# Twenty-four short products of constant tiles placed among the first two attention jobs

## The chip, the cores and the metric

The kernel runs on one core of a Trainium2 chip. A core has five engines that run side by side, each through its own instructions in order: TensorE (PE, with its weight loads as PEld), VectorE (DVE), ScalarE (ACT), GpSimd (POOL) and SyncE (SP, which sends DMAs here). The metric is the time of one execution on the device in microseconds (us). The median of three timed runs of the kernel before is 696.04 us (694.4 to 696.12).

## The reference

Three layers follow each other:

```
# 1. attention, q, k, v: (2 batches, 8 heads, 576 positions, 64)
q_d, k_d, v_d = means over 4 neighbouring positions          # 144 positions
out = repeat(softmax(q_d k_d^T / 8) v_d, 4)                  # coarse part
    + softmax(q k^T / 8 where |i - j| < 4) v                 # band part
x = out as (1152 tokens, 512)
# 2. h = x @ w_in (512 x 2048);  x = (h * sigmoid(h)) @ w_out (2048 x 512)
# 3. p = domain_probs normalized over 4 experts
out = sum over e of p[:, e] * (relu(x @ w1[e]) @ w2[e])      # w1 512 x 1024, w2 1024 x 512
```

Everything is float32.

## The kernel before

**Work and stages.** Attention is cut into 16 jobs: 2 batches x 2 column blocks (`c`: 256 or 320 positions) x 4 pairs of heads (`hp`). A job j runs through these helpers: `local_scores` (band scores in windows of 64 positions, L318, and a product of a small identity `ident16` with the constant `mask`, L324, that adds the mask), `local_max` and `local_exp` (L331, L332, L336), `pool_kq_first` for the first four jobs (four products with `ident` that sum neighbouring keys into `kd`, L282, copied out by ACT, L285), `down_scores` (L342), `down_max` (L356 to L358), `norm` (L363 to L368), `trans` (transposes of both weights, L378 and L380), `values` (L406, L410, then L413 and L415) and `split_x` (L422, L423), which writes the job's part of x as an upper and a lower half, `xh` and `xl`. The tile `ps` of a job is one PSUM bank and holds both its kinds of scores.

The second layer, `g1_step` and `g2_step`, multiplies halves: xh by the upper weights, xl by the upper, xh by the lower (`mm3`, L485). The first three products over tokens of the first block are begun while attention still runs (`start_mm`, in PSUM tiles `hold`, of which it uses columns 0 to 255). The third layer (L673 to L719) follows.

**Weights.** The weights of the second layer come in eight units of four pieces of 512 KB. SP loads a piece into one of three stage buffers (`load_raw`, L154); `split_raw` takes it apart into two halves with ACT (L179, L180, L187), DVE (L181, L185) and POOL (L188), and frees the buffer. The splits of unit 1 are tied behind L423 of job 2, those of units 2 and 3 behind L423 of job 3 (`behind_job`).

**What sets the order.** The code issues steps by ticks (`plan_jobs`): job k starts at tick -18 + 3k; its down scores come 2 ticks later, its transposes 5, its values 6, its split 7. Each instruction gets a priority from its tick, and a scheduler with a model of times then writes each engine's order. `follow(i, earlier, ...)` adds an edge that keeps i behind `earlier` in that order, without a semaphore when both are on one engine; `after` is `follow` for two products in one PSUM bank.

Of the kernel before, what the change touches and what calls it, by code (L numbers as in the profile page):

```python
# [9 lines left out]
F32 = mybir.dt.float32  # L10
# [11 lines left out]
HP = NH // 2  # L22
# [4 lines left out]
WIN = BQ + 6  # L27
# [14 lines left out]
HOLD = 3  # L42
# [17 lines left out]
def attention_moe_kernel(ctx, tc, kqa, kqb, qtl, va, vb, w64, w1d, w2d, dpr, out):  # L60
    nc = tc.nc
    PE, ACT, DVE, POOL, SP = nc.tensor, nc.scalar, nc.vector, nc.gpsimd, nc.sync

    const = ctx.enter_context(tc.tile_pool(name="const", bufs=1))
    mm_p = ctx.enter_context(tc.tile_pool(name="mm", bufs=3, space=PSUM))
# [46 lines left out]
    def follow(i, earlier, reason):  # L112
        tc.add_manual_dep(i.ins, earlier.ins.name, mybir.DependencyInfo(mybir.DependencyClass.NoSync, mybir.DependencyReason.DATA),
                          reason=reason)
# [77 lines left out]
            behind(DVE, DVE.tensor_tensor(out=l[:, c], in0=t, in1=h[:, c].bitcast(F32), op=ALU.subtract))  # L192


    actx = ExitStack()
    ac = actx.enter_context(tc.tile_pool(name="ac", bufs=1))
    a2 = actx.enter_context(tc.tile_pool(name="a2", bufs=2))
# [5 lines left out]
    ident = ac.tile([128, 128], F32, name="ident")  # L203
    ident16 = ac.tile([128, 128], BF16, name="ident16")
    mask = ac.tile([128, 6, WIN], BF16, name="mask")
# [71 lines left out]
    def pool_kq_first(j):  # L277
        kp = j.ps[:, 352:352 + SD]
        kd[j.b, j.hp] = a4.tile([128, SD], F32, tag="kd", name="kd")
        k4 = j.k[:, 3:3 + S].rearrange("p (n r) -> p n r", r=4)  # L280
        for r in range(4):
            i = PE.matmul(out=kp, lhsT=ident, rhs=k4[:, :, r], start=(r == 0), stop=(r == 3))  # L282
            if r == 0:
                after(i, j.group)
        ACT.activation(out=kd[j.b, j.hp], in_=kp, func=ACTF.Copy)  # L285
        j.qd = qbd[j.hp % 2]
        q4 = j.q[:, 0:256].rearrange("p (n r) -> p n r", r=4)
        for h in range(2):
            p = slice(64 * h, 64 * h + 64)
            DVE.tensor_reduce(out=j.qd[p, h], in_=q4[p], axis=AX.X, op=ALU.add)  # L290
# [16 lines left out]
    def after(i, earlier):  # L307
        follow(i, earlier, "PSUM bank")

    def local_scores(j):  # L310
        nb = j.nb
        j.ps = s_p.tile([128, 512], F32, tag="s", name="s")
        mk = mask[:, 0:4] if j.c == 0 else mask[:, 1:6]
        first = [None, None]
        for m in range(nb):
            for h in range(2):
                p = slice(64 * h, 64 * h + 64)
                i = PE.matmul(out=j.ps[p, m * WIN:(m + 1) * WIN], lhsT=j.q[p, 64 * m:64 * m + 64],  # L318
                              rhs=j.k[p, 64 * m:64 * m + WIN], start=(m == 0), stop=False, skip_group_check=True)
                if m == 0:  # L320
                    first[h] = i
                else:
                    after(i, first[h])
        j.group = PE.matmul(out=j.ps[:, 0:nb * WIN], lhsT=ident16, rhs=mk.rearrange("p m c -> p (m c)"),  # L324
                            start=False, stop=True, skip_group_check=True)

    def local_max(j):
        nb = j.nb
        j.st = a2.tile([128, 20], F32, tag="st", name="st")
        j.lo = j.ps[:, 0:nb * WIN].rearrange("p (m c) -> p m c", c=WIN)  # L330
        DVE.tensor_reduce(out=j.st[:, 0:nb], in_=j.lo, axis=AX.X, op=ALU.max)  # L331
        DVE.tensor_tensor(out=j.lo, in0=j.lo, in1=j.st[:, 0:nb].unsqueeze(2).to_broadcast([128, nb, WIN]), op=ALU.subtract)  # L332
# [8 lines left out]
    def down_scores(j):  # L341
        i = PE.matmul(out=j.ps[:, 352:352 + SD], lhsT=j.qd.rearrange("p a b -> p (a b)"), rhs=kd[j.b, j.hp],  # L342
                      start=True, stop=True)
        after(i, j.group)

    def tail_scores(l):
        l.ps = s_p.tile([128, 512], F32, tag="s", name="s")
        for hp in range(HP):
            PE.matmul(out=l.ps[32 * hp:32 * hp + 32, 352:352 + SD], lhsT=qdl[:, hp].rearrange("p a b -> p (a b)"),
                      rhs=kd[l.b, hp], start=True, stop=True, tile_position=(0, 32 * hp))  # L350
        l.st = a2.tile([128, 20], F32, tag="st", name="st")
# [18 lines left out]
    def trans(j):  # L370
        nb = j.nb
        if j.c == 1 and j.hp == 0:
            atd[j.b] = ac.tile([72, 2, NH, 80], F32, tag="atd1", name="atd1")
        t1 = t_p.tile([128, 4, 128], F32, tag="t1", name="t1")
        t2 = t_p.tile([128, 4, 128], F32, tag="t2", name="t2")
        j.at = ac.tile([WIN, 5, 128], F32, tag="at", name="at")
        for m in range(nb):
            PE.transpose(t1[0:WIN, m] if m < 4 else t2[0:WIN, 0], j.sm[:, m, :], ident)  # L378
        for kh in range(2):
            PE.transpose(t2[0:72, 1 + kh], j.ed[:, 72 * kh:72 * kh + 72], ident)  # L380
        ACT.activation(out=j.at[:, 0:4], in_=t1[0:WIN], func=ACTF.Copy)
        if nb == 5:
            ACT.activation(out=j.at[:, 4], in_=t2[0:WIN, 0], func=ACTF.Copy)
            dst = atd[j.b][:, :, 2 * j.hp:2 * j.hp + 2, 0:64]
        else:
            j.atd = ac.tile([72, 2, 2, 64], F32, tag="atd0", name="atd0")
            dst = j.atd
        ACT.activation(out=dst, in_=t2[0:72, 1:3].rearrange("p a (h q) -> p a h q", h=2), func=ACTF.Copy)
# [94 lines left out]
    def mm3(ps, pairs, first, last):  # L483
        n = len(pairs)
        ins = [PE.matmul(out=ps, lhsT=l, rhs=r, start=(first and i == 0), stop=(last and i == n - 1))  # L485
               for i, (l, r) in enumerate(pairs)]
        return ins[0], ins[-1]

    def g1_pairs(u0, ft, k, c):
        wh, wl = unit[u0 + ft // 4]  # L490
        s = slice(k * 512 + (ft % 4) * 128, k * 512 + (ft % 4) * 128 + 128)
        return [(wh[:, s], xh[:, k, c]), (wh[:, s], xl[:, k, c]), (wl[:, s], xh[:, k, c])]
# [8 lines left out]
    def g1_evac(ps, ft, n):  # L501
# [9 lines left out]
            latest[DVE] = DVE.tensor_tensor(out=gl[ft][:, 0:n], in0=gf[:, 0:n], in1=gh[ft][:, 0:n].bitcast(F32), op=ALU.subtract)  # L511

        pend.append(fin)

    def mm_tile():
        return mm_p.tile([128, 512], F32, tag="mm", name="mm")

    def g1_step(u0, ft, ci):
        n = XN[ci]
        c = slice(XOFF[ci], XOFF[ci] + n)  # L520
        ps = mm_tile()
        for k in range(HP):
            mm3(ps[:, 0:n], g1_pairs(u0, ft, k, c), k == 0, k == HP - 1)
        g1_evac(ps, ft, n)
# [230 lines left out]
            store(t)  # L755


    hold = []

    def start_mm(hp):  # L760
        for i in range(HOLD):
            if hp == 0:
                hold.append(mm_tile())
            mm3(hold[i][:, 0:256], g1_pairs(0, i, hp, slice(0, 256)), hp == 0, hp == HP - 1)

    main_parts.append(start_mm)
    plan_jobs()
    for hp in range(HP):
        at_tick(FIRST + PER * hp + 8, 9, start_mm, hp)
# [177 lines left out]
```

## Time and profile before

| what | value |
|---|---|
| median of 3 timed runs | 696.04 us |
| the profiled execution | 690.55 us, span 688.6 us |
| PE busy | 657.6 us (95% of the span) |
| DVE, ACT, POOL busy | 440.6, 330.8, 245.9 us |

The profiled execution is one run; its span goes from the first to the last instruction, and about 2 us lie around it. Start times are counted from the start of the span. PE's products of float32 stand as two records each. The records of PE overlap, since a product's end reaches into the next one's start; how dense a run is shows in the distance of starts.

### The profile page before, as it was taken

The page shows a single profiled execution, that of the slowest core. Times are in us where ns is not written, and L with a number is a line of the kernel's source. Part 1 is how long each engine was busy: PE and PEld are TensorE (multiplying, and loading weights), DVE is VectorE, ACT ScalarE, POOL GpSimd, SP SyncE. Part 2 cuts the span into 40 slices and gives each one's busy share as a digit, 9 for nine tenths or more (in the row PEclk, how much of TensorE's full clock was granted, in tenths as well). Part 3 has the DMA queues.
Part 4 walks back from the last instruction along what each step waited for, and adds up shares of the span by engine and source line. Part 5 has one row for each costly group of instructions (what it writes and reads, how often), then busy time and mean ns, then how long its engine had stood idle before and what let it go on. Part 6 is the DMA issues. An engine that isn't in the chain of part 4 may idle for free.

```text
span 688.6 us, 13803 instructions
## 1 busy us (share of the span) xinstructions
PE 657.6 (95%) x5516; PEld 640.3 (93%) x5516; DVE 440.6 (64%) x882; ACT 330.8 (48%) x753; POOL 245.9 (36%) x346
## 2 busy tenths in 40 slices
PE   5877899999999999999999999999999999999996
PEld 4667779999999999999999999999999999999996
DVE  5579978556753643785476875558954669755444
ACT  4659667556752632543335643346533355433321
POOL 5344771123330000453265433455422654332210
PEclk9999999999999999999999999999999999999999
DMA  9656562015230300050002420003210010000001
GB/s 283 196 174 194 179 198 66 23 56 177 77 121 1 110 15 1 1 189 27 1 2 62 123 62 1 2 18 106 93 31 1 1 62 1 1 32 23 10 31 46
DMA packets 16927, 48.16 MB, mean 70 GB/s; under 512 B 2976, under 2 KB 4256, under 8 KB 16864
## 3 DMA queue, kind: packets, MB, share of 16 engines
q1 hardware_dynamic: 16864, 47.29, 22.2%
q8 instruction: 43, 0.70, 0.4%
q14 instruction: 20, 0.16, 0.1%
HBM read 44.93 MB, written 2.36 MB: 69 GB/s over the span
## 4 chain that ended last, share of the span: by engine, by line
PE 82%; DVE 8%; DMA 5%; ACT 3%; issue 2%; SPq 0%; POOL 0%; ACTq 0%; DVEq 0%
PE mm L485 50%; PE p L691 26%; DMA stg<-in_w_dram 5%; DVE dec L181 2%; DVE dec L185 2%; DVE gl L511 1%; PE s L318 1%; PE t L378 1%; ACT stg L180 1%; PE o L410 1%; PE s L282 1%; PE s L342 1%; PE o L406 1%; DVE acc L719 1%; ACT dec L179 1%
## 5 line engine op out<-in xcount | busy, mean ns | idle before, releaser
L485 PE MATMUL mm<-xh,wbuf 128*128 128x256 f32 (+2 forms) x1280 | 265.0, 294 | 4.3 <-ACT xh L422 2.6
L485 PEld LDWEIGHTS mm<-xh,wbuf 128*128 128x128 f32 x1280 | 208.9, 188 | 5.6 <-ACT xh L422 3.3
L485 PE MATMUL mm<-xl,wbuf 128*128 128x256 f32 (+2 forms) x640 | 188.4, 295 | 0.0
L673 POOL TENSOR_TENSOR r<-r 128x128 f32<-128x128 f32 x160 | 93.4, 595 | 186.2 <-ACT r L667 144.6
L676 DVE TENSOR_TENSOR h<-r,h 128x384 fp32r<-128x384 f32 (+1 forms) x128 | 91.6, 718 | 67.3 <-ACT h L675 67.1
L485 PEld LDWEIGHTS mm<-xl,wbuf 128*128 128x128 f32 x640 | 120.8, 189 | 0.1
L675 ACT ACTIVATE h<-r 128x384 fp32r<-128x384 f32 (+1 forms) x128 | 73.3, 578 | 91.9 <-POOL r L673 54.2
L485 PE MATMUL mm<-gh,wbuf 128*128 128x256 f32 (+1 forms) x512 | 106.3, 299 | 3.5 <-DVE gf L505 2.1
L691 PE MATMUL p<-wext,h 128*128 128x256 f32 x672 | 92.6, 281 | 0.0
L485 PEld LDWEIGHTS mm<-gh,wbuf 128*128 128x128 f32 x512 | 83.3, 189 | 4.9 <-DVE gf L505 2.5
L691 PE MATMUL p<-wbuf,h 128*128 128x256 f32 x672 | 86.0, 281 | 0.0
L691 PEld LDWEIGHTS p<-wext,h 128*128 128x128 f32 x672 | 85.4, 189 | 0.0
L691 PEld LDWEIGHTS p<-wbuf,h 128*128 128x128 f32 x672 | 82.5, 188 | 0.0
L485 PE MATMUL mm<-gl,wbuf 128*128 128x256 f32 (+1 forms) x256 | 74.9, 297 | 0.4 <-DVE gl L511 0.4
L673 DVE TENSOR_TENSOR r<-r 128x128 f32<-128x128 f32 x96 | 39.8, 415 | 38.2 <-ACT r L667 33.6
L667 ACT ACTIVATE r<-mm 128x512 f32<-128x512 f32 x48 | 28.5, 596 | 72.9 <-PE mm L485 72.6
L485 PEld LDWEIGHTS mm<-gl,wbuf 128*128 128x128 f32 x256 | 48.4, 190 | 0.7 <-DVE gl L511 0.7
L511 DVE TENSOR_TENSOR gl<-gf,gh 128x256 fp32r<-128x256 f32 (+1 forms) x64 | 34.2, 540 | 16.9 <-ACT gh L510 16.6
L188 POOL TENSOR_TENSOR wbuf<-dec,wbuf 128x512 fp32r<-128x512 f32 x24 | 32.2, 1348 | 30.7 <-ACT wbuf L187 20.2
L618 POOL TENSOR_TENSOR wext<-kst,wext 128x512 fp32r<-128x512 f32 x8 | 10.3, 1291 | 83.2 <-ACT wext L616 44.9
L719 DVE SCALAR_TENSOR_TENSOR acc<-p,pr,acc 128x256 f32<-128x256 f32 (+1 forms) x63 | 36.1, 605 | 4.9 <-PE p L691 4.9
L505 DVE SCALAR_TENSOR_TENSOR gf<-th,mm 128x256 f32<-128x256 f32 (+1 forms) x64 | 28.4, 448 | 16.7 <-ACT th L504 14.9
(122 smaller groups left out, 971.8 us busy)
## 6 DMA issues: line engine op xcount, KB each, us to landing
stg<-in_w_dram SPq DMA_DIRECT2D x32, 512.0 KB, 3.8
kst<-in_w2d_dram SPq DMA_DIRECT2D x16, 512.0 KB, 3.7
kst<-in_w1d_dram SPq DMA_DIRECT2D x12, 512.0 KB, 3.7
kq<-in_kqa_dram SPq DMA_DIRECT2D x8, 419.0 KB, 3.6
kq<-in_kqb_dram SPq DMA_DIRECT2D x8, 323.0 KB, 9.9
vg<-in_va_dram SPq DMA_DIRECT2D x8, 288.0 KB
stg<-in_w1d_dram SPq DMA_DIRECT2D x4, 512.0 KB
vw<-in_vb_dram SPq DMA_DIRECT2D x8, 180.0 KB
```

The lines of the kernel that those rows point to most:

```text
L181: i = DVE.scalar_tensor_tensor(out=ai, in0=ai, scalar=3, in1=v[:, :, 0], op0=ALU.logical_shift_left, op1=ALU.bitwise_or)
L185: DVE.scalar_tensor_tensor(out=ai, in0=v[:, :, 1], scalar=-2 ** 31, in1=ai, op0=ALU.bitwise_and, op1=ALU.bitwise_or)
L188: POOL.tensor_tensor(out=l[:, c], in0=a, in1=h[:, c].bitcast(F32), op=ALU.subtract)
L485: ins = [PE.matmul(out=ps, lhsT=l, rhs=r, start=(first and i == 0), stop=(last and i == n - 1)) for i, (l, r) in enumerate(pairs)]
L505: DVE.scalar_tensor_tensor(out=gf[:, 0:n], in0=th[:, 0:n], scalar=1.0, in1=ps[:, 0:n], op0=ALU.add, op1=ALU.mult)
L511: latest[DVE] = DVE.tensor_tensor(out=gl[ft][:, 0:n], in0=gf[:, 0:n], in1=gh[ft][:, 0:n].bitcast(F32), op=ALU.subtract)
L667: ACT.activation(out=r[:, 0:4].rearrange("p s t -> p (s t)"), in_=ps[:, 0:512], func=ACTF.Relu)
L673: latest[eng] = eng.tensor_tensor(out=r[:, o], in0=r[:, a], in1=r[:, b], op=op)
L675: ACT.activation(out=h, in_=r[:, part], func=ACTF.Copy)
L676: latest[DVE] = DVE.tensor_tensor(out=l, in0=r[:, part], in1=h.bitcast(F32), op=ALU.subtract)
L691: ins = [PE.matmul(out=ps, lhsT=x, rhs=y, start=(opens and k == 0 and i == 0), stop=(k == 3 and i == n - 1), skip_group_check=True) for i, ...
L719: DVE.scalar_tensor_tensor(out=o, in0=ps, scalar=p, in1=o, op0=ALU.mult, op1=ALU.add)
```

## The change

A function `fill(i, n)` issues n products of `ident16` (the weights) with 256 columns of the mask, all bfloat16, into columns 256 to 511 of the first `hold` tile, which nothing reads. Each is ordered behind the one before, the first behind the product `i`. It is called at five places: behind job 0's mask product (4), job 1's sums of keys (5), job 0's down scores (3), job 1's down scores (8), job 0's transposes (4). Job 0's down scores, its first transpose and the first product of `start_mm` are ordered behind the last filler issued till then. The `hold` tiles are now taken at the first filler.

```
+    hold, filled = [], []
+
+    def fill(i, n):
+        if not hold:
+            hold.extend(mm_tile() for _ in range(HOLD))
+        for _ in range(n):
+            f = PE.matmul(out=hold[0][:, 256:512], lhsT=ident16, rhs=mask.rearrange("p m c -> p (m c)")[:, 70:326],
+                          start=True, stop=True)
+            follow(f, i, "filling")
+            i = f
+        filled[:] = [i]
...
         ACT.activation(out=kd[j.b, j.hp], in_=kp, func=ACTF.Copy)
+        if j.i == 1:
+            fill(i, 5)
...
         j.group = PE.matmul(out=j.ps[:, 0:nb * WIN], lhsT=ident16, rhs=mk.rearrange("p m c -> p (m c)"),
                             start=False, stop=True, skip_group_check=True)
+        if j.i == 0:
+            fill(j.group, 4)
...
         after(i, j.group)
+        if j.i == 0:
+            follow(i, filled[0], "filling")
+        if j.i < 2:
+            fill(i, (3, 8)[j.i])
...
-            PE.transpose(t1[0:WIN, m] if m < 4 else t2[0:WIN, 0], j.sm[:, m, :], ident)
+            i = PE.transpose(t1[0:WIN, m] if m < 4 else t2[0:WIN, 0], j.sm[:, m, :], ident)
+            if j.i == 0 and m == 0:
+                follow(i, filled[0], "filling")
         for kh in range(2):
-            PE.transpose(t2[0:72, 1 + kh], j.ed[:, 72 * kh:72 * kh + 72], ident)
+            i = PE.transpose(t2[0:72, 1 + kh], j.ed[:, 72 * kh:72 * kh + 72], ident)
+        if j.i == 0:
+            fill(i, 4)
...
-    hold = []
-
     def start_mm(hp):
         for i in range(HOLD):
-            if hp == 0:
-                hold.append(mm_tile())
-            mm3(hold[i][:, 0:256], g1_pairs(0, i, hp, slice(0, 256)), hp == 0, hp == HP - 1)
+            m = mm3(hold[i][:, 0:256], g1_pairs(0, i, hp, slice(0, 256)), hp == 0, hp == HP - 1)
+            if hp == 0 and i == 0:
+                after(m[0], filled[0])
```

The orders below count instructions of the program; lines behind L193 are higher by 3 to 29 in the changed kernel (L282 is L285 there, L324 is L343, L342 is L363, L378 and L380 are L403 and L407, L406 and L410 are L435 and L439, L485 is L514; on DVE L356 is L381, L415 is L444, L423 is L452).

PE around the down scores of jobs 0 and 1 (`qbd_116` and `qbd_117`), before:

```order
L324 MATMUL s<-mask,ident_114 128x280
L282 MATMUL s<-kq,ident 128x144 x8
L342 MATMUL s<-kd,qbd_116 128x144
L342 MATMUL s<-kd,qbd_117 128x144
L378 MATMUL t_228<-ident,sm 70x128 x4
```

And in the changed kernel, where the pair of L323 stands four times in a row at the first "..." and eight times at the second:

```order
L343 MATMUL s<-mask,ident_114 128x280
L323 LDWEIGHTS ident_114
L323 MATMUL mm<-mask,ident_114 128x256
...
L343 LDWEIGHTS ident_114
L343 MATMUL s<-mask,ident_114 128x280
L285 MATMUL s<-kq,ident 128x144 x8
L363 MATMUL s<-kd,qbd_116 128x144
L323 LDWEIGHTS ident_114
L323 MATMUL mm<-mask,ident_114 128x256
...
L363 MATMUL s<-kd,qbd_117 128x144
L403 MATMUL t_243<-ident,sm 70x128 x4
```

Four fillers stand between the two mask products, and eight (the three behind job 0's down scores and job 1's five) between the two down scores.

PE behind job 0's second transposes (`t_229`) up to job 2's down scores (`qbd_116` again), before; `t_311` and `t_312` are job 1's transposes, `atd_238` belongs to job 0's values:

```order
L380 MATMUL t_229<-ident,ed 72x128 x2
L378 MATMUL t_311<-ident,sm 70x128 x4
L318 MATMUL s<-kq 64x70 x8
L324 MATMUL s<-mask,ident_114 128x280
L406 MATMUL o<-atd_238,vd 64x64 x4
L410 MATMUL o<-at,vw 64x64 x3
L282 MATMUL s<-kq,ident 128x144 x4
L410 MATMUL o<-at,vw 64x64 x5
L380 MATMUL t_312<-ident,ed 72x128 x2
L342 MATMUL s<-kd,qbd_116 128x144
```

In the changed kernel (`t_244`, `t_338` and `t_339`, `atd_257` are the same tiles), with the pair of L323 twelve times:

```order
L407 MATMUL t_244<-ident,ed 72x128 x2
L323 LDWEIGHTS ident_114
L323 MATMUL mm<-mask,ident_114 128x256
...
L435 MATMUL o<-atd_257,vd 64x64 x4
L439 MATMUL o<-at,vw 64x64 x8
L285 MATMUL s<-kq,ident 128x144 x4
L403 MATMUL t_338<-ident,sm 70x128 x4
L337 MATMUL s<-kq 64x70 x6
L407 MATMUL t_339<-ident,ed 72x128 x2
L514 MATMUL mm<-xh,wbuf 128x256 x3
L514 MATMUL mm<-xl,wbuf 128x256
L363 MATMUL s<-kd,qbd_116 128x144
```

The last twelve fillers come first, then job 0's values and job 2's sums of keys; job 1's transposes stand behind these, and nine products of the second layer (`xh` and `xl`) now come ahead of job 2's down scores.

DVE around the third L423 (job 2's `xl`) and the first split of unit 1, before:

```order
L415 TENSOR_TENSOR o<-o,od 128x256
L356 TENSOR_REDUCE st<-s 128x1
L331 TENSOR_REDUCE st<-s 128x5
L357 TENSOR_SCALAR st<-st 128x1
L423 TENSOR_TENSOR xl<-o,xh 128x256
L181 SCALAR_TENSOR_TENSOR dec<-dec,stg_328 128x512
```

And in the changed kernel:

```order
L392 TENSOR_TENSOR sm<-s,st 128x280
L444 TENSOR_TENSOR o<-o,od 128x256
L452 TENSOR_TENSOR xl<-o,xh 128x256
L352 TENSOR_REDUCE st<-s 128x5
L181 SCALAR_TENSOR_TENSOR dec<-dec,stg_428 128x512
```

The three instructions of jobs 3 and 5 that stood between the sum of the two parts and the split of job 2's x stand elsewhere now.

## Rows read from the trace of the kernel before

**Rows 1.** The page: busy time by engine, and slices of the span.

```profile
PE 657.6 (95%) x5516; PEld 640.3 (93%) x5516; DVE 440.6 (64%) x882; ACT 330.8 (48%) x753; POOL 245.9 (36%) x346
...
PEclk9999999999999999999999999999999999999999
```

**Rows 2.** Stretches of PE: from:to, length, busy (records), granted clock, DMA share, GB/s.

```profile
4.38:7.20 2.82, 2.79 (x34) 1.00 1.00 381
...
8.30:12.80 4.50, 4.45 (x16) 1.00 1.02 257
12.80:19.00 6.20, 1.70 (x4) 1.00 1.01 337
24.00:31.70 7.70, 7.70 (x59) 1.00 0.48 153
44.80:48.80 4.00, 0.83 (x5) 1.00 0.74 217
48.80:52.20 3.40, 3.39 (x21) 0.50 0.57 183
69.20:72.70 3.50, 3.50 (x21) 0.51 0.29 110
95.00:160.00 65.00, 63.83 (x660) 1.00 0.24 70
```

**Rows 3.** PE in order of time: start, length, instruction, idle time before.

```profile
8.32 4.45 PE L282 MATMUL s<-kq,ident 128*128 128x144 f32 x16 [1.15 <-DVE s L332]
14.40 0.85 PE L342 MATMUL s<-kd,qbd 128*128 128x144 f32 x2 [1.63 <-ACT s L336]
19.04 1.07 PE L378 MATMUL t<-ident,sm 128*70 128x128 f32 x4 [2.23 <-DVE sm L367]
21.17 0.41 PE L324 MATMUL s<-mask,ident 128*128 128x280 bf16 x1
23.05 1.04 PE L378 MATMUL t<-ident,sm 128*70 128x128 f32 x4 [1.05 <-DVE sm L367]
32.20 0.42 PE L342 MATMUL s<-kd,qbd 128*128 128x144 f32 x2
34.35 0.28 PE L485 MATMUL mm<-xl,wbuf 128*128 128x256 f32 x1
34.47 0.28 PE L485 MATMUL mm<-xh,wbuf 128*128 128x256 f32 x1
35.61 0.60 PE L378 MATMUL t<-ident,sm 128*70 128x128 f32 x4
```

**Rows 4.** The chain of waits: start, length, what.

```profile
13.40 0.66 ACT stg L180
...
23.05 1.04 PE t L378 x4
...
32.38 0.26 PE s L342 x2
...
45.92 3.90 DMA stg<-in_w_dram
...
80.58 6.75 DMA stg<-in_w_dram
```

**Rows 5.** DVE in order of time.

```profile
17.76 0.30 DVE L356 TENSOR_REDUCE st<-s 128x1 f32<-128x144 f32 x1
...
40.77 0.43 DVE L415 TENSOR_TENSOR o<-o,od 128x256 f32<-128x256 f32 x1 [1.81 <-ACT od L413]
...
42.37 0.41 DVE L423 TENSOR_TENSOR xl<-o,xh 128x256 fp32r<-128x256 f32 x1
```

**Rows 6.** Waits of SP's queue, 0 to 60 us: total, times, longest.

```profile
SPq L154 <- DVE dec L185: 19.7, 9, 3.9
```

**Rows 7.** Stretches of DVE, columns as in rows 2.

```profile
60.00:80.00 20.00, 19.93 (x39) 0.91 0.52 157
80.00:95.00 15.00, 12.07 (x30) 1.00 0.82 248
```

More of the change, by code (lines that the diff above doesn't have):

```diff
@@ L192, in split_raw, with mm_tile @@
             behind(DVE, DVE.tensor_tensor(out=l[:, c], in0=t, in1=h[:, c].bitcast(F32), op=ALU.subtract))
+    def mm_tile():
+        return mm_p.tile([128, 512], F32, tag="mm", name="mm")
     actx = ExitStack()
@@ L513, in g1_evac @@
         pend.append(fin)
-    def mm_tile():
-        return mm_p.tile([128, 512], F32, tag="mm", name="mm")
     def g1_step(u0, ft, ci):
```

## Prediction

> **What bounds the kernel now.** I read the page first, then stretches of PE, then the chain of waits, then DVE and SP around one instruction. On the page PE is busy 95% of the span [rows 1], and the stretches show where the rest lies: from 95 us on PE is all but full (63.83 of 65 us to 160) [rows 2]. So the end of the kernel is set by when that dense part starts, and every microsecond by which the first 95 us become shorter is one off the end, unless a wait there takes it.
>
> The clock of PE in this first part has to be read from durations. The page's slices show a granted clock of full speed from the start [rows 1], but nothing shows that this is a record and not a default: the product of L342 takes 0.85 us for its two records at 14.40, and 0.42 us at 32.20 [rows 3]. [...] Before it rose, PE had been busy without a gap from 24.00 to 31.70. Before that it had a gap of 1.15 us ahead of L282, was busy only 1.70 of 6.20 us from 12.8 to 19 and waited again ahead of both L378; the 4.45 us of L282 in between didn't raise it [rows 2, 3]. It falls once at 48.8, after a stretch in which PE was busy 0.83 of 4.00 us, and once at 69.2; each time the granted clock is about half for 3.4 us [rows 2].
>
> On the chain of waits the time from 23.05 to 32.64 is PE, piece after piece (ten pieces, the first and the last shown; 9.59 us), all at the lower clock. Up to 23 us the chain runs over a weight transfer that lands at 13.40 and then over DVE [rows 4]. After it, the third job's lower half of x (L423 at 42.37) releases the splits of the second unit of weights (L181, tied behind it by `behind_job`), these free the stage buffers (L185), and only then SP sends the next weight transfer, which the chain shows at 45.92 [rows 4, 5]. SP's weight transfers waited 19.7 us in nine pieces for L185 [rows 6]. I call the end of that L423, 42.78, the pivot: what lies behind it (DVE is busy 19.93 of 20 us at 60 to 80 [rows 7]) moves with it.
>
> **The change part by part.** It adds 24 products (4+8+12 as PE's order has them), each with a weight load, and removes nothing; the scheduler then also gives PE, DVE, ACT, POOL and SP another order for the jobs behind.
>
> *One filler.* The trace has no 128x256 bf16 product. From below: in a dense run at the higher clock, records of 256 columns start 0.12 us apart (34.35 and 34.47) [rows 3]; at half the clock that is 0.24. From above: a lone 128x280 bf16 product takes 0.41 us [rows 3]. Fillers stand in runs of 4, 8 and 12 with one weight tile, so I take 0.12 and 0.24 us; 24 of them are 2.9 to 5.8 us of PE, and at the upper bound 9.8.
>
> *The first four* stand between the two jobs' mask products. 4 x 0.24 = 1.0 us, in a place where PE waits 1.15 us for DVE's L332 [rows 3]. Job 1's subtraction comes up to 1.0 us later, but its exp waits behind an ACT instruction that only starts at 13.40, when a weight transfer lands [rows 4]. Cost: nothing; without that cover 1.0.
>
> *The next eight* stand between the two down scores: 8 x 0.24 = 1.9 us from about 15.1, so job 1's down score starts near 17.0 and ends near 17.9. DVE, which has other work till then, would take its maximum at 17.76 [rows 5]. Cost: 0.2, since L367 of job 0 stands behind that maximum on DVE.
>
> *The last twelve* stand behind job 0's second transposes, one wait ahead of job 1's at 23.05, and hold up all of PE behind them: job 0's values, job 2's sums of keys, job 1's transposes. At the lower clock they take 12 x 0.24 = 2.9 us, of which 1.05 us is the wait for DVE's L367 that stands there anyway [rows 3]: cost 1.8. At the higher one 1.4 us: 0.4. If the clock is up by 19 us, the transposes and scores ahead are done sooner and it is about 0. I take 0.9.
>
> *The clock.* What they can bring is an earlier rise. With them the gap of 1.15 us ahead of L282 is filled. PE then works from the first scores (2.79 of 2.82 us from 4.38 on) to L282's end at 12.77: over 8 us, against the 7.7 us of full work before the rise in this trace [rows 2, 3]. If this isn't enough, the 12 in a row at 22 us follow on 3 us of work, and there the rise should come by about 25 us. With the rise before 23 us the 9.59 us at the lower clock halve: -4.8; with it at 25 us only the last 7.6 of them do: -3.8.
> [...]
>
> *The order.* Between job 2's down score (32.20) and the pivot (42.78) lie 10.6 us, though PE runs at the higher clock there. PE put job 3's transposes and scores of job 5 ahead of job 2's values, and DVE put three instructions between L415 (40.77) and L423 (42.37) [rows 5]. In the new order job 2's values stand ahead of both, and L423's successor follows directly on L415's. Against that nine products of L485 now stand ahead of job 2's down score: 9 x 0.12 = 1.1 us. Removed ahead of the values are four transposes (0.60, as at 35.61) and eight scores that I put at the same [rows 3]; on DVE most of the 1.2 us between the two goes. I take -1.1, between +2 (the nine at 0.24, nothing won on DVE) and -4 (the values as early again as PE's waits there allow).
>
> *Sum* for the pivot: 0 + 0.2 + 0.9 - 4.8 - 1.1 = -4.8. Behind it the chain still has waits for weight transfers (the first is 3.90 at 45.92, the longest 6.75 at 80.58) [rows 4]. They are sent when DVE frees a buffer, so they move along; DMA is busy 0.52 to 0.82 of these stretches [rows 7], so they find room. The profiled execution took 690.55 (span 688.6), which gives 685.75. The three timed runs have a median of 696.04, 5.5 above; I carry the difference over to that: 691.2.
>
> **The rivals.**
> *The rise is lost again, or comes only in the third group.* After the first run PE again has little to do from 17 to 19 us, and in this trace the clock did fall after a thin stretch (0.83 of 4.00) [rows 2]. Against it: the fillers raise 1.70 of 6.20 to about 3.6. The twelve then run at the lower clock (+1.8), a part of the 9.59 stays there (-3.8 instead of -4.8) and the order brings half (-0.5), with 0.2 as above: -2.3, 693.7.
> [...]
>
> *The gain is taken by a wait behind the pivot.* DVE is full from 60 to 80 us [rows 7]; SP's transfers of v and k for later jobs are tied to POOL and PE work that doesn't get faster. For it: the weight transfer of 6.75 us, long for 512 KB beside 3.90, in a stretch with DMA at 0.82. Against: what DVE does there starts with the pivot. If all but a microsecond of it is lost: 695.
>
> *Slower: the fillers don't raise the clock* (the change then doesn't do what it says). The place is PE from 22.0 to 33 us: twelve fillers cost 1.8 us, at the lone product's 0.41 us 3.9; the nine products ahead of job 2's down score cost 9 x 0.24 = 2.2. That is +4.0 to +6.1, less 1.2 that the order saves elsewhere: 2.8 to 4.9 more, some 699.5. It decides if the rise comes at 31 us or later, as now. Against it stands the gapless run, which would be longer than the one that raised the clock before.
>
> **How the numbers follow.** Main case 0.52, 688 to 693 by its own terms; clock lost or late 0.18; taken behind the pivot 0.17; slower 0.13. A change within 0.3% (2.1 us) can't be told from none here. Faster (below 693.9): the main case and five sixths of the second, 0.67; same: the rest of the second and the third, 0.20; slower 0.13. Range: the low end is the main case with the order at its best (-1.1 becomes -4) and the fillers free, 687; the high end leaves out the slower case's upper part, 697.5.
>
> **What would show it.** In the trace after: L342's successor (now L363) takes 0.42 instead of 0.85 us in the first two jobs, or at the latest the four transposes of job 1 take 0.60 instead of 1.04; the pieces from job 1's transposes to job 2's down score need 5 us, not 9.6; the third L423 ends near 38 instead of 42.78; the dense part starts near 90. Wrong would be: a cold 0.85 at all three; the third L423 early but the transfers behind it landing where they did; a fall of the clock between 20 and 35 us; or the twelve fillers with PE's values waiting for nothing else behind them.

## The result, and the profile after

The changed kernel takes 697.87 us (median of 15 runs, 695.4 to 701.55) against 694.5 for the kernel before beside it (15 runs, 690.11 to 696.12): a ratio of 1.0064, 95% interval 1.0047 to 1.008. It is slower by 0.6%, and outside the range that was forecast. The profiled execution took 698.2 us, span 696.2. Between the two profiles lie 7.6 us and between the medians 3.4, because the profiled 690.55 of before was among its fastest; so the experiments below are judged by their timed ratios, and profiles are used for places.

The page of the changed kernel (called after below), busy time and granted clock by slices, answers to [rows 1]:

```profile
PE 665.1 (96%) x5540; PEld 645.4 (93%) x5540; DVE 446.5 (64%) x882; ACT 331.6 (48%) x753; POOL 250.1 (36%) x346
...
PEclk9888789999999999999999999999999999999998
```

PE is busy 7.5 us longer. The granted clock is below nine tenths in five of the first six slices. Stretches of PE in after, columns as in [rows 2], cut where the granted clock changes:

```profile
8.77:15.59 6.82, 4.94 (x23) 1.00 1.04 265
15.59:22.42 6.83, 4.41 (x32) 0.53 1.00 313
22.42:46.31 23.89, 20.97 (x244) 0.99 0.56 164
46.31:56.55 10.24, 7.85 (x42) 0.52 0.66 215
56.55:70.21 13.66, 11.78 (x138) 0.98 0.59 173
70.21:80.45 10.24, 8.91 (x70) 0.52 0.57 176
80.45:94.10 13.65, 10.24 (x124) 0.98 0.62 182
94.10:100.93 6.83, 5.19 (x45) 0.53 0.61 197
```

The rise comes at 8.8 us, where it came near 32 in the profile of the kernel before (the records of the clock begin there, at 8.8 and 31.7 us, and read full), is lost from 15.6 to 22.4, and then holds to 46.3. Behind that the clock falls three times, for 10.2, 10.2 and 6.8 us, where before it fell twice for 3.4 [rows 2]. PE in order of time, as in [rows 3] (L285 is L282, L363 is L342, L403 is L378):

```profile
7.04 1.06 PE L323 MATMUL mm<-mask,ident 128*128 128x256 bf16 x4
...
8.28 4.56 PE L285 MATMUL s<-kq,ident 128*128 128x144 f32 x16
14.71 0.51 PE L363 MATMUL s<-kd,qbd 128*128 128x144 f32 x2 [1.88 <-ACT s L357]
15.06 1.04 PE L323 MATMUL mm<-mask,ident 128*128 128x256 bf16 x8
16.30 0.85 PE L363 MATMUL s<-kd,qbd 128*128 128x144 f32 x2 [0.20 <-ACT s L357]
...
22.13 1.85 PE L323 MATMUL mm<-mask,ident 128*128 128x256 bf16 x12
...
24.77 2.30 PE L285 MATMUL s<-kq,ident 128*128 128x144 f32 x8
26.89 0.62 PE L403 MATMUL t<-ident,sm 128*70 128x128 f32 x4
```

The fillers cost what was forecast for one (four start 0.21 us apart, since the next product starts at 7.89; eight take 1.04 us, twelve 1.85). The first down score is at the higher clock, the second at the lower again (0.85), and job 1's transposes take 0.62 us as hoped. DVE, third and ninth L423 (L452 here), with the idle time before:

```profile
39.37 0.42 DVE L452 TENSOR_TENSOR xl<-o,xh 128x256 fp32r<-128x256 f32 x1 [0.82 <-ACT xh L451]
...
104.67 0.42 DVE L452 TENSOR_TENSOR xl<-o,xh 128x256 fp32r<-128x256 f32 x1 [1.30 <-ACT xh L451]
```

The ninth in the kernel before:

```profile
97.46 0.42 DVE L423 TENSOR_TENSOR xl<-o,xh 128x256 fp32r<-128x256 f32 x1 [0.45 <-ACT xh L422]
```

The pivot ends at 39.79, 3.0 us ahead of the 42.78 of [rows 5]. But the ninth job's L423 ends at 105.09, where it ended at 97.88 before: the lead has become a lag of 7.2 us, and that lag stays to the end (the spans differ by 7.6). The chain of after, as in [rows 4], shows what lies between:

```profile
44.60 4.37 DMA stg<-in_w_dram
...
83.23 2.77 DVE dec L181
86.02 1.02 DVE dec L185
87.09 4.17 DMA stg<-in_w_dram
...
95.74 1.07 PE t L403 x4
```

The first weight transfer behind the pivot starts 1.3 us earlier than the one at 45.92 and takes 0.5 longer. Later a split of 2.77 us on DVE (L181, which takes 0.68 us at 57.37), a transfer and the ninth job's transposes stand on the chain. Around these, PE in before and then in after:

```profile
79.26 0.41 PE L342 MATMUL s<-kd,qbd 128*128 128x144 f32 x2
...
86.16 0.63 PE L378 MATMUL t<-ident,sm 128*70 128x128 f32 x4 [0.17 <-DVE sm L367]
```

```profile
87.75 0.38 PE L514 MATMUL mm<-gh,wbuf 128*128 128x256 f32 x1 [1.64 <-ACT wbuf L187]
89.71 1.06 PE L363 MATMUL s<-kd,qbd 128*128 128x144 f32 x4
...
95.74 1.07 PE L403 MATMUL t<-ident,sm 128*70 128x128 f32 x4 [1.83 <-DVE sm L392]
```

The ninth job's down scores come at 79.3 in before and at 89.7 in after, its transposes at 86.2 and 95.7. That is the new order at work, so the first question was which part of the change costs: the order, or the fillers and the clock.

### The profile page after: what moved, and what is told of

The parts are those of the page before. It is cut to its first block, busy times and chain, and to the rows that moved or that the text cites. A ratio compares the mean times of both kernels' runs of the same rounds, so it can differ in the third digit from the quotient of the medians.

```text
span 696.2 us, 13842 instructions
## 1 busy us (share of the span) xinstructions
PE 665.1 (96%) x5540; PEld 645.4 (93%) x5540; DVE 446.5 (64%) x882; ACT 331.6 (48%) x753; POOL 250.1 (36%) x346
## 4 chain that ended last, share of the span: by engine, by line
PE 86%; DVE 6%; DMA 3%; ACT 2%; issue 1%; SPq 0%; POOL 0%; ACTq 0%; DVEq 0%
PE mm L514 53%; PE p L717 26%; DMA stg<-in_w_dram 3%; PE s L337 2%; DVE dec L181 1%; DVE gl L540 1%; PE t L403 1%; DVE dec L185 1%; PE o L439 1%; PE o L435 1%; PE s L285 1%; PE t L407 1%; DVE acc L745 1%; PE s L343 1%; ACT dec L179 0%
## 5 line engine op out<-in xcount | busy, mean ns | idle before, releaser
L514 PE MATMUL mm<-xh,wbuf 128*128 128x256 f32 (+2 forms) x1280 | 267.3, 296 | 3.6 <-DVE gf L534 1.9
L514 PEld LDWEIGHTS mm<-xh,wbuf 128*128 128x128 f32 x1280 | 210.9, 190 | 4.5 <-DVE gf L534 2.6
L514 PE MATMUL mm<-xl,wbuf 128*128 128x256 f32 (+2 forms) x640 | 188.6, 295 | 0.0
L514 PEld LDWEIGHTS mm<-xl,wbuf 128*128 128x128 f32 x640 | 121.6, 190 | 0.3 <-DVE xl L452 0.2
L514 PE MATMUL mm<-gh,wbuf 128*128 128x256 f32 (+1 forms) x512 | 107.7, 302 | 5.1 <-ACT wbuf L187 2.4
L514 PEld LDWEIGHTS mm<-gh,wbuf 128*128 128x128 f32 x512 | 84.1, 191 | 6.9 <-ACT wbuf L187 3.1
L514 PE MATMUL mm<-gl,wbuf 128*128 128x256 f32 (+1 forms) x256 | 75.1, 298 | 1.1 <-DVE gl L540 1.1
L540 DVE TENSOR_TENSOR gl<-gf,gh 128x256 fp32r<-128x256 f32 (+1 forms) x64 | 39.7, 625 | 16.7 <-ACT gh L539 16.3
L514 PEld LDWEIGHTS mm<-gl,wbuf 128*128 128x128 f32 x256 | 48.5, 190 | 1.5 <-DVE gl L540 1.5
L188 POOL TENSOR_TENSOR wbuf<-dec,wbuf 128x512 fp32r<-128x512 f32 x24 | 32.3, 1351 | 28.4 <-ACT wbuf L187 17.4
L644 POOL TENSOR_TENSOR wext<-kst,wext 128x512 fp32r<-128x512 f32 x8 | 10.3, 1291 | 83.2 <-ACT wext L642 44.6
L534 DVE SCALAR_TENSOR_TENSOR gf<-th,mm 128x256 f32<-128x256 f32 (+1 forms) x64 | 28.6, 450 | 16.4 <-ACT th L533 14.9
```

The source lines that it names most:

```text
L188: POOL.tensor_tensor(out=l[:, c], in0=a, in1=h[:, c].bitcast(F32), op=ALU.subtract)
L534: DVE.scalar_tensor_tensor(out=gf[:, 0:n], in0=th[:, 0:n], scalar=1.0, in1=ps[:, 0:n], op0=ALU.add, op1=ALU.mult)
L644: b = eng.tensor_tensor(out=l[:, r], in0=x, in1=h[:, r].bitcast(F32), op=ALU.subtract)
```

## The experiments

**The order and the fillers apart.** All kernels here but the changed one run again have each engine's order written out, by edges between neighbours:

```
+    def order_as(table):
...
+            for x, y in zip(line, line[1:]):
+                tc.add_manual_dep(y, x.name, mybir.DependencyInfo(mybir.DependencyClass.NoSync, mybir.DependencyReason.DATA),
+                                  reason="order")
...
     finish(*before, tick_of(NE, 0, 0) + 2)
+    order_as(ORDER)
```

`ORDER` lists each engine's instructions by their number in the order of issue (`374+4` is four from 374). The first kernel is the one before with the table of the changed one, the second the changed one with the table of before and the fillers behind the same instructions, the third the changed one unaltered. A line of the first one's table (POOL):

```
-        "23 30+2 24+2 36+3 63 32+3 41+3 35 47+3 39 64 40 70 44 53 55 45 54 56+2 71 "
+        "27 36+3 29+3 33 32 63 34+2 41+3 47 39 48+2 64 40 70 44 71 45 77 46 53 "
```

For the second, PE's line gets the fillers (`F4`, `F8`, `F12`):

```
-        "0+8 14+8 8 22 9+4 23+4 13 33 27+4 46+9 31+2 59+4 87+9 34+7 55+4 41+5 63+2 96+4 65+2 69 "
+        "0+8 14+8 8 F4 22 9+4 23+4 13 F8 33 27+4 46+9 31+2 F12 59+4 87+9 34+7 55+4 41+5 63+2 "
```

The order alone: 

> The changed kernel's order on all five engines, written out as edges, with the 24 fillers left out; every other instruction as before. Theory 1 (the order that the scheduler made around the fillers costs the time, the fillers themselves help or are free): slower than before by 3 to 5 us, as the changed kernel or more. Rival (the fillers' effect on the clock costs it: an early rise is followed by more stretches at the lower level): within 1 us of before, and the granted clock of the profile near 0.99, as before.

The fillers alone: 

> The order of before on all five engines, written out as edges, with the 24 fillers put behind the same three instructions as in the changed kernel (4, 8, 12). Theory 1 (order): faster than before by 2 to 5 us, since the products of the first jobs run at the higher clock and nothing else moves. Rival (clock): slower by 3 us or more, with a granted clock near 0.97 as in the changed kernel's profile.

The changed kernel again: 

> The changed kernel once more, on the same chip as the two others: both theories expect 3.4 us more than before (697.9 against 694.5), and a granted clock near 0.97.

Measured: the order alone 698.34 us, ratio 1.0082 (1.0052 to 1.0112). The fillers alone 694.57, ratio 1.0027 (1.0004 to 1.005). Both, 697.73, ratio 1.0071 (1.0042 to 1.01). The order costs all of it; the fillers bring nothing on either order. That the fillers alone aren't faster goes against what was expected of them, 2 to 5 us less. Why not, with the clock up? PE of the kernel with the fillers alone (L417 is L282, L536 is L378, L496 is L342), at a clock that was full from 22 to 42 us:

```profile
23.43 0.60 PE L536 MATMUL t<-ident,sm 128*70 128x128 f32 x4
...
25.43 2.30 PE L417 MATMUL s<-kq,ident 128*128 128x144 f32 x8
...
28.40 2.21 PE L417 MATMUL s<-kq,ident 128*128 128x144 f32 x8
30.43 0.42 PE L496 MATMUL s<-kd,qbd 128*128 128x144 f32 x2
...
41.53 0.51 PE L496 MATMUL s<-kd,qbd 128*128 128x144 f32 x2 [2.49 <-POOL qbd L390]
```

And the same sums of keys in the kernel before, at the lower clock; the two transposes between them take 0.64 us, against 0.41 at the higher clock, and the rise comes during or behind the second piece:

```profile
26.54 2.40 PE L282 MATMUL s<-kq,ident 128*128 128x144 f32 x8
...
29.70 0.64 PE L380 MATMUL t<-ident,ed 128*72 128x128 f32 x2
30.14 2.24 PE L282 MATMUL s<-kq,ident 128*128 128x144 f32 x8
```

These sums take the same time at either level (so do the sixteen records of the first two jobs: 4.45 us in [rows 3], 4.56 in after with the clock up from 8.77), though transposes and down scores nearly halve. Down scores have the same shape, 128x144, but read `kd` without gaps, while L282 reads every fourth key (`k4[:, :, r]`); whether that is the reason no run shows. From job 1's transposes to job 2's down score PE needs 7.4 us (23.43 to 30.85) instead of 9.6. Of these 2.2 us nothing arrives: PE then waits 2.49 us for POOL, which sums a later job's queries (`qbd`), and the third L423 ends at 43.51, between the 42.78 and 44.64 of two profiles of the kernel before.

**Which stretch of the order.** Four mixtures: up to a cut in time (on all engines, closed under what waits for what) one kernel's table, behind it the other's. POOL's line in the first of them against the changed kernel:

```
-        "27 36+3 29+3 33 32 63 34+2 41+3 47 39 48+2 64 40 70 44 71 45 77 46 53 "
+        "27 36+3 29+3 33 32 63 34+2 41+3 47 39 48+2 64 40 70 44 71 45 53 55 54 "
```

New order to 79 us, with fillers: 

> The changed kernel (all 24 short products in place) with its own order on all engines up to about 79 us, and the order of the kernel before for everything behind. Theory A (what costs is the order behind 79 us, where PE takes the down scores of the ninth and tenth job at 89 us instead of 79 and 85, behind 17 products that wait for weights and behind the eighth job's values): the ninth job's L423 ends at 96 to 99 us instead of 104.6, products of L485 behind it start as before, and the time is 691 to 694.5, 3 us or more below the changed kernel's 697.8. Theory B (the loss is made ahead of 79 us, in the new order's waits among weight transfers and splits, and only shows later): 696.5 to 698.5, as the changed kernel. Theory C (the lower clock among 45 and 100 us is the price): the clock is as low as in the changed kernel, mean 0.965 to 0.98, and the time stays above 696.

The same without: 

> As the run before this one, without the 24 short products. Theory A: 692.5 to 695, about the kernel before's time (694.5); what the products bring on top of it is the difference to the run before this one, at most 1.5 us. Theory B: 697 to 699, as the new order alone (698.3). Theory C: below 696 if its mean clock is above 0.98, else as B.

The other way round, against the kernel before (POOL):

```
-        "58 60 46 59 50 61+2 77+2 51 65 67 52 66 68+2 72 74 82 73 75+2 83+4 79+3 "
+        "77 46 58 60 50 78 59 61+2 51 82 52 83 65 67 66 68+2 72 74 84 73 "
```

> The kernel before, with its own order up to about 79 us on all engines, and the changed kernel's order for everything behind; no short products. Theory A: 698 to 701, slower than the kernel before by as much as the new order alone or more, and the ninth job's L423 ends at 103 us or later. Theory B: 693 to 695.5, as the kernel before. Theory C: it goes with the clock, below 695.5 at a mean of 0.985 or more.

New order to 44 us only, against the changed kernel (POOL):

```
-        "27 36+3 29+3 33 32 63 34+2 41+3 47 39 48+2 64 40 70 44 71 45 77 46 53 "
+        "27 36+3 29+3 63 32+3 41+3 35 47+3 39 64 40 70 44 53 55 45 54 56+2 71 58 "
```

> The changed kernel (all 24 short products) with its own order only up to about 44 us, and the order of the kernel before for everything behind. If the lead of 3 us that the third L423 has (39.4 instead of 42.8) can be carried to the end: 691 to 692.5, below the run that keeps the new order to 79 us. If the stretch from 44 to 90 us, where splits on DVE and weight transfers release each other, takes the lead whatever the order: 693 to 695, equal to the kernel before, and the ninth job's L423 ends at 97 to 98 us as before.

Two more at the early cut, and the kernel before again, with its own order written out as edges. New order to 44 us, no fillers (the table of the run just named, without `F4`, `F8` and `F12`): 

> The kernel before with the changed kernel's order up to about 44 us and its own order behind, no short products. Against the run with them (695.75) it gives the products' price under this order. If they cost PE their own time and bring nothing (24 products, 3 us): 692 to 694.5, and with the lead that the new order itself has at the third L423 perhaps below the kernel before (693.5). If the earlier rise of the clock pays for them: 695 to 697.

New order behind 47 us, against the kernel before (POOL):

```
-        "23 30+2 24+2 36+3 63 32+3 41+3 35 47+3 39 64 40 70 44 53 55 45 54 56+2 71 "
+        "23 30+2 24+2 36+3 33 32 63 34+2 41+3 47 39 48+2 64 40 70 44 71 45 77 46 "
```

> The kernel before with its own order up to about 47 us (the end of its third job's second transposes and values) and the changed kernel's order for all behind, no short products. If the loss is made behind 44 us (the second layer's gate pieces L505 and L511 ahead of the seventh job's attention pieces on DVE at 55 to 70 us, and POOL's wait for a transfer of v ahead of the ninth job's keys at 80 us): 698 to 701, the ninth job's L423 at 104 us or later. If it is made ahead of that: 693 to 695.

Before, its own order: 

> The kernel before, unchanged, once more with a profile: 690 to 698. If the milestones behind 44 us (the ninth job's L423 at 97.9 in the first profile) are the program's and not of one execution, they come within 2 us of those, and the share of the lower clock may differ without moving them by more than 2 us.

The measurements so far, with three readings of each profile: the ends of the third L423, the time from the sixth L423 to the seventh and from the eighth to the ninth, and the granted clock from 44 to 105 us.

| order to 44 / to 79 / behind | fillers | us | ratio (95%) | third | 6th-7th | 8th-9th | clock |
|---|---|---|---|---|---|---|---|
| old / old / old (first profile) | no | 694.5 | 1 | 42.78 | 7.4 | 4.1 | 0.94 |
| old / old / old (as edges) | no | 692.72 | 0.9997 (0.9966-1.0028) | 44.64 | 6.8 | 5.5 | 0.94 |
| old / old / old | 24 | 694.57 | 1.0027 (1.0004-1.005) | 43.51 | 8.2 | 6.1 | 0.84 |
| new / old / old | no | 693.61 | 1.0029 (1.0009-1.005) | 39.66 | 7.2 | 4.7 | 0.83 |
| new / old / old | 24 | 695.75 | 1.0027 (1.0006-1.0048) | 41.66 | 7.2 | 4.7 | 0.83 |
| new / new / old | no | 696.98 | 1.004 (1.0012-1.0067) | 42.18 | 12.6 | 5.3 | 0.80 |
| new / new / old | 24 | 698.45 | 1.0056 (1.0029-1.0083) | 41.55 | 11.6 | 4.9 | 0.83 |
| new / new / new | no | 698.34 | 1.0082 (1.0052-1.0112) | 39.37 | 11.0 | 12.7 | 0.75 |
| new / new / new (changed) | 24 | 697.87 | 1.0064 (1.0047-1.008) | 39.79 | 10.3 | 11.4 | 0.78 |
| new / new / new (changed, again) | 24 | 697.73 | 1.0071 (1.0042-1.01) | 39.44 | 10.2 | 12.2 | 0.72 |
| old / new / new | no | 700.3 | 1.011 (1.0083-1.0136) | 43.78 | 9.6 | 13.0 | 0.81 |
| old / old / new | no | 703.73 | 1.0145 (1.0116-1.0174) | 42.81 | 13.8 | 12.1 | 0.75 |

Medians come from different chips; the ratios are to the kernel before on the same one. The second row shows no cost of the edges themselves (0.9997). Three things stand in this table. The lead at the third L423 is the order's, not the clock's: without fillers it ends at 39.37, 39.66 and 42.18 with the new start and at 42.78 to 44.64 with the old one, 3 us apart on average, though one order alone spreads over 2 to 3 us. And the lead doesn't reach the end: with the old order behind it the kernel is still 0.3% slower than before. The loss is made behind 44 us: the old start with the new rest costs 1.1%. And the two delays go with their stretch: from 8th to 9th 11 to 13 us wherever the new order stands behind 79 us and 4.1 to 6.1 elsewhere, from 6th to 7th 9.6 us and more with the new order from 44 to 79 us, or with the seam at 79, and up to 8.2 elsewhere. Theory A was right on the step from the eighth job to the ninth, and wrong on the place of the ninth (106.09, expected at 96 to 99) and on the time (698.45 where it said 691 to 694.5), because the middle stretch loses too; the mixtures' losses don't add up either, since the old order to 79 with the new one behind is the slowest of all.

Some expectations were missed. The new order to 44 us with fillers took 695.75, above both its ranges (up to 695). The new order to 79 without fillers took 696.98, between its two ranges and next to theory B's. The old order to 79 with the new one behind took 703.73, above the 701 of theory A. And the kernel before itself has its ninth L423 at 99.94 in the second profile, 2.06 us behind the first.

The whole difference is made ahead of the end of the ninth L423. It comes between 97.88 and 112.33 us in the fourteen profiles of these kernels, those of the two sections below included, and from there to the end of the profiled execution all of them take the same, 590.8 to 593.9 us (592.67 in before, 593.11 in after).

What the stretch costs on the engines: DVE from 44 to 105 us in before, in after, with the new order to 44 us (with fillers) and with the old order to 47 us, one line of each:

```profile
44.00:105.00 61.00, 52.18 (x117) 0.94 0.63 190
```

```profile
44.00:105.00 61.00, 50.60 (x102) 0.78 0.61 186
```

```profile
44.00:105.00 61.00, 49.61 (x112) 0.83 0.62 190
```

```profile
44.00:105.00 61.00, 52.13 (x106) 0.81 0.60 184
```

DVE is nearly as busy and gets through 102 records instead of 117. In the five profiles with the old order behind 44 us they are 108 to 118, in all others 98 to 107. Part of that is length: L511 and L505 (L540 and L534 in after), eight of each shape in that stretch, from DVE's groups by form (busy time, mean ns, idle time) in before and in after:

```profile
L511 DVE TENSOR_TENSOR gl<-gf,gh 128x256 fp32r<-128x256 f32 x8 | 4.9, 618 | 0.0
L505 DVE SCALAR_TENSOR_TENSOR gf<-th,mm 128x256 f32<-128x256 f32 x8 | 3.2, 406 | 0.7 <-ACT th L504 0.7
```

```profile
L540 DVE TENSOR_TENSOR gl<-gf,gh 128x256 fp32r<-128x256 f32 x8 | 8.2, 1029 | 0.1
L534 DVE SCALAR_TENSOR_TENSOR gf<-th,mm 128x256 f32<-128x256 f32 x8 | 3.3, 414 | 0.1
```

The long ones lie beside POOL's additions. DVE in after, and POOL at the same time:

```profile
62.72 1.15 DVE L540 TENSOR_TENSOR gl<-gf,gh 128x256 fp32r<-128x256 f32 x1
...
65.31 2.00 DVE L540 TENSOR_TENSOR gl<-gf,gh 128x256 fp32r<-128x256 f32 x1
...
68.05 0.41 DVE L540 TENSOR_TENSOR gl<-gf,gh 128x256 fp32r<-128x256 f32 x1
```

```profile
62.30 1.29 POOL L188 TENSOR_TENSOR wbuf<-dec,wbuf 128x512 fp32r<-128x512 f32 x1
...
64.56 1.20 POOL L258 TENSOR_TENSOR vd<-vg 72x256 f32<-72x256 f32 x1 [0.15 <-PE o L435]
65.71 1.31 POOL L188 TENSOR_TENSOR wbuf<-dec,wbuf 128x512 fp32r<-128x512 f32 x1
```

The two long ones end 0.3 us behind an L188 that ran beside them; the one with POOL idle takes 0.41. L505, one of whose inputs lies in PSUM, has nearly the same length in both kernels (406 and 414 ns). What makes L511 longer beside POOL no row shows. Across runs the mean varies (841 ns in the second profile of the changed kernel, 748 in before's), so this is a part of the loss and not its measure. Over all of DVE's records from 44 to 105 us, what they take beyond the shortest record of the same operation and shape adds up to 10.4 to 11.5 us in the five profiles with the old order behind 44 us and to 12.0 to 15.6 in the nine others: 3 us more on average. Among the nine it doesn't follow the loss, and how much of it reaches the end isn't shown.

**The ninth job alone.** In the changed kernel POOL sums the pieces of a v (waiting 4.23 us for its transfer) and does weight additions ahead of the ninth job's keys. Moving this one job up:

```
-        "27 36+3 29+3 33 32 63 34+2 41+3 47 39 48+2 64 40 70 44 71 45 77 46 53 "
-        "55 58 60 50 78 54 56+2 59 61+2 51 82 52 83 65 67 66 68+2 72 74 84 "
+        "27 36+3 29+3 33 32 63 34+2 41+3 47 39 48+2 64 40 70 44 71 45 53 55 54 "
+        "56+2 77 46 58 60 50 78 59 61+2 51 82 52 83 65 67 66 68+2 72 74 84 "
```

> The changed kernel with one job's pieces moved up in its order, all else as it is: POOL takes the ninth job's sums of keys and its qbd ahead of the transfer of v that it waits for at 80 us, PE takes that job's down scores ahead of the 17 products that wait for weights at 84 us and its transposes and values ahead of where they stand at 95 to 102 us, DVE and ACT take its maximum, exp and norm before the eighth job's second half of x. If the late ninth job is where the time goes (theory A): PE's waits at 86 to 95 us are filled, the ninth job's L423 comes 2 us or more earlier than 104.6, PE has some 20 products of L485 more done at 105 us than the changed kernel, and the time is 694 to 696.5, 1.5 to 4 us below the changed kernel's 697.8. If the ninth job is only a sign, and what counts is how much PE gets done by 95 us under the lower clock and beside the splits: 697 to 698.5.

Measured: 703.36 us, ratio 1.0142 (1.0114 to 1.0171), worse than either expectation; the ninth L423 ends at 110.60. POOL, ACT and DVE of this kernel (L287 is L179, L296 is L188, L289 is L181) show a reason:

```profile
84.92 1.26 POOL L296 TENSOR_TENSOR wbuf<-dec,wbuf 128x512 fp32r<-128x512 f32 x1
```

```profile
86.21 0.67 ACT L287 ACTIVATE dec<-stg 128x512 f32<-128x512 f32 x1 [2.03 <-POOL wbuf L296]
```

```profile
86.92 2.06 DVE L289 SCALAR_TENSOR_TENSOR dec<-dec,stg 128x512 int32<-128x512 int32 x1 [3.26 <-ACT dec L287]
```

POOL's addition, now behind the keys, frees the buffer that ACT's split waits for, and DVE waits for ACT. In this stretch the jobs and the splits share DVE, ACT and POOL, and what the one gets earlier the other gets later. So the late ninth job looks like a sign of the order; this move, at least, didn't mend it.

**The clock kept up.** 82 more of the short products, in PE's own waits:

```
+    def late(t, n):
+        for _ in range(n):
+            f = PE.matmul(out=t[:, 256:512], lhsT=ident16, rhs=late_rhs, start=True, stop=True, skip_group_check=True)
...
+            if here:
+                late(ps, {2: 12, 4: 8, 6: 11, 7: 5}.get(f, 0))
```

> The changed kernel with 82 more short products of the same kind on PE, in its own waits behind 42 us (7, 11, 9 and 7 at 42 to 51 us, 12 at 69, 8 at 77, 11 at 87, 5 at 92, 12 at 95 us), each run some 80% of the wait that it fills at 0.12 us a product. They are to keep the clock up where the changed kernel's fell for 10 us at a time. The first thing to see is the granted clock from 44 to 105 us: 0.78 in the changed kernel, above 0.9 if they work. Theory C (the lower clock of that stretch is the price of the new order): with the clock up 690 to 694.5, as fast as the kernel before or faster. Theory B (the splits, DVE and POOL set the pace from 44 to 95 us, and PE's clock there costs at most 1 or 2 us): 696 to 699.5 with the clock up.

This kernel doesn't compute the reference's result, and the added products write into PSUM banks in which sums of the second layer are being formed; its other instructions are the changed kernel's, in the same order, and only its time is read. PE's stretch, where after has a granted clock of 0.78:

```profile
44.00:105.00 61.00, 49.42 (x502) 0.92 0.57 179
```

Measured: 700.24 us, ratio 1.0099 (1.0061 to 1.0137), the mean clock of every timed run between 0.982 and 0.991 where the changed kernel's were 0.967 to 0.981. (These means take what lies ahead of the first record of the clock as full: the two profiles of the kernel before have 0.994 and 0.982, and both 0.94 from 44 to 105 us.) With the clock back up the time is no shorter, and 0.7 us above the range of theory B. Alone this doesn't settle theory C, since the 82 products have a price of their own: some 75 of the 502 records are theirs, so PE has done about 430 of its own, where the changed kernel's two profiles have 465 and 454. The table says the same from the other side. At nearly one clock, 0.81 to 0.84, the ratios run from 1.0027 to 1.011 with the order, and with the old order behind 44 us a clock of 0.83 or 0.84 instead of 0.94 goes with 0.3%. So theory C falls as the account of the loss; whether a small part of it is the clock's isn't shown.

## Why the prediction was wrong

**The step that failed is "the order"**, together with the sentence that all behind the pivot moves with it. The step gave -1.1 (from +2 to -4) for the way to the pivot. There it was right in sign and inside its bounds, though small: with no filler at all the new order brings the pivot from 43.5 (mean of four profiles without fillers) to 40.4 (mean of three), -3.1. But it was counted only up to there, and no term stood for the order of the sixty microseconds behind, in which every engine's list was altered; of the transfers there the sum says only that they move along and find room. That order costs 1.1% by itself (about 7.6 us), and with its own start 0.8%, where the sum has nothing. The orders of the two kernels showed this before the run: POOL's place of the ninth job's keys and PE's of its down scores could have been read from them.

**The clock, -4.8.** The mechanism came as forecast (a rise before 23 us, lost for 6.8 us and regained), the size did not. In the seven profiles with fillers the clock is up to stay from 22 to 26 us, in the seven without from 27 to 33. The first rise, lost again, isn't the fillers' alone: in the second profile of the kernel before the first two down scores take 0.51 us (at 13.65 and 15.22), where the first of them took 0.85 in [rows 3]; its granted clock (0.89 from 0 to 105 us, 0.76 from 24 to 44, 0.94 from 44 on) comes to some 0.87 ahead of 24, where the first profile's reads full. So it came at different moments in two executions of one program. That the 9.59 us halve no run shows: 4.36 of them are sums of keys on the chain (two pieces of L282, 2.33 and 2.03), which take 2.2 to 2.4 us at both levels. The last of the ten pieces, L342 at 32.38, was at the higher clock already. With the order of before the stretch shrank by 2.2 us, and even these were then spent in the wait of 2.49 us for POOL's sums of queries. The range had no bound for it: the trace of before shows no sum of keys that is known to be at the higher clock, and the gain should have been bounded below by nothing. Four transposes, on the other hand, take 1.07 us at the lower clock and 0.60 to 0.62 at the higher.

**The fillers, 0 + 0.2 + 0.9.** One filler at 0.12 to 0.24 us was right (1.06, 1.04 and 1.85 us for four, eight and twelve, each with the tail of its last record). With and without them the kernels can't be told apart: 1.0071 and 1.0082 on the new order, 1.0027 and 1.0029 with it to 44 us, 1.0056 and 1.004 to 79. Only on the old order do they cost 0.27%, with an interval that nearly reaches zero.

**The rivals.** The rise lost again did happen, and no run gives it a price of its own. That the gain is taken by a wait behind the pivot is the nearest: DVE is as full as it said (19.89 of 20 us from 60 to 80 in after), but it expected the gain gone, and here a lead of 3.0 us at the pivot became a lag of 7.2 at the ninth L423. The slower rival had the right sign by a wrong mechanism, since the fillers do raise the clock; its place was PE from 22 to 33 us, and the loss is made behind 44. Its time, some 699.5, is near the measured 697.87 by luck. The upper end of the range, 697.5, left out not the upper part of this rival but all of it: by its own terms it gives 698.8 to 700.9. And the base of the sum, 696.04, was a median of three runs; fifteen gave 694.5.

**What would show it.** Job 1's transposes took 0.62 us, and the clock didn't fall from 22.4 to 46.3, so the signs of the clock came. The third L423 came early, and the first weight transfer with it (44.60 instead of 45.92); but PE still waits 1.83 us ahead of the transposes at 95.74 and is busy without a gap only from 100.9 on, where the dense part was to start near 90. Watching the pivot alone would have called the change a success.

**What stays open.** How the 0.8% splits between DVE's longer instructions, POOL's order, the transfers and perhaps the clock isn't settled: one engine's order can't be exchanged alone, since the lists of the five depend on each other, and the mixtures have seams of their own.

## What to carry to other kernels

When a change makes a scheduler write a new order, follow each engine's new list to the point where the work is dense again, and price it there; a milestone halfway can be 3 us early and the end 4 us late. Before a faster clock is counted, look for the same instruction at both levels (the same shape isn't enough: down scores and sums of keys are both 128x144, and only the down scores halve, 0.85 to 0.42 us, where the sums take 2.40 and 2.21), and for the next engine's readiness. Where splits, jobs and transfers release each other on three engines, ask of a late piece that is to be moved up whose place it takes; here moving one cost 0.7% more. And before a low clock is called the price, compare kernels at the same clock.

## What was not expected of the hardware

- Products of L282 (128x144, float32, eight records) take 2.40 us at the lower clock and 2.21 and 2.30 at the higher, while the transposes (1.07 and 0.60) and down scores (0.85 and 0.42) beside them halve or nearly halve.
- A DVE subtraction of 128x256 takes 0.41 us with POOL idle and 1.15 or 2.00 us beside POOL's additions, ending just behind them.
- With PE's clock from 44 to 105 us at 0.72 to 0.94, the time goes with the order and hardly with the clock: at 0.81 to 0.84 the ratios run from 1.0027 to 1.011.
- The first rise of the clock falls differently in two executions of the same instructions in the same order: the first down score of the kernel before takes 0.85 us at 14.40 in one profile and 0.51 us at 13.65 in the other.
